# Attention, gated MLP and routed attention on one core: the first transfers in another order

## The chip, the cores and the metric

The kernel runs on one core of a Trainium2 chip. The metric is the device time of one execution in microseconds (us). Engines are named as in the profile: PE (TensorE, matmuls), DVE (VectorE), ACT (ScalarE), POOL (GpSimd) and SP, whose queue issues all transfers between HBM and the on-chip memory.

## The reference

Three layers follow one another on a batch of 2 with 448 positions. Cut to what matters:

```python
# 1. causal attention, 12 heads of width 64
scores = q @ k.T / 8, masked above the diagonal
x = softmax(scores) @ v                      # heads side by side: (2, 448, 768)
# 2. gated MLP
h = gelu(x @ w_in)                           # 1024 columns
u, v = h[..., :512], h[..., 512:]
v = layernorm(v) * g_ln
x = x + (u * (w_sg @ v + b_sg)) @ w_out
# 3. 4 attention experts of width 64, each position takes 2 of them
out = sum over e of gate[e] * softmax(causal(x wq[e] (x wk[e]).T / 8)) (x wv[e]) wo[e]
```

## The kernel before, in words

The first layer works on pairs of heads: 24 heads (two batches of 12) make 12 pairs. `qk_load` (L716) asks for q and then k of one pair, 224 KB each, into rings of two buffers per name (`qraw`, `kraw`). `qk_trans` (L728) copies such a buffer into a `pair` tile in another order (DVE, POOL or ACT, L378 to L382), and four transposes on PE (L737) turn it; the result is copied out of its PSUM bank as `qt` or `kt`. `scores1` (L771) multiplies qt and kt for both heads, in two banks per head (L782: 12 matmuls for the first bank of the pair in the trace, 8 for the second). `bank_chain` then runs per head and bank: mask, minimum and scaling on DVE (L434, into `tm` and `bias`), the exponential with its row sums on ACT (L444, into `p` and `sm`), a small step on POOL (L450), the reciprocal on DVE (L452), the scaling of p on POOL (L458) or DVE (L456), four transposes on PE (L462), and a copy into `pt` (L378 or L380). `pair_chain` multiplies pt with v for the pair (L504, 28 matmuls, called AV here) and splits the result into xh and xl.

v comes in groups of four heads, `v_group` (L700): two transfers of 64 KB (L704, L706) and three of 128 KB (L709) into one of three `v_raw` buffers. The weights of the MLP's u half come in eight transfers of 384 KB (`w_u`, L644, into three `raw` buffers); each is converted from 64-bit words to float (ACT L651, POOL L654, DVE L656 and L658) and split into a high and a low part, `wuh` and `wul` (L378 to L385). The matmuls with them (`u_chain`, L866) serve as filler on PE between the steps of the attention. Later come the v half of the MLP, the spatial product, the output product, and the third layer. `load_halves` (L877) loads g_half and b_half, which POOL scales (L885, L886).

No order is written out by hand. A planner (`class Order`, L118) runs at build time: each step names what it needs, what buffers it takes and an estimated cost; `o.add(rank, ...)` starts a chain with a rank, and among the steps that can start at about the same planned time on an engine the one of lowest rank is issued. The planner's choice fixes every engine's instruction order and, where a step allows several engines, the engine. A `need` is a condition of the planner; on the chip an instruction waits only for the data and buffers that it uses, and a transfer also for the landing of the transfer eight places ahead of it on SP's queue. The ranks of the first transfers are `4 * p + R["load"]` (that is 4p - 37) for pair p, `EARLY` (-22) for the first three weights of u, and `V0` (-4) for v's first group.

Of the kernel before, what the change touches and what calls it, by code (L numbers as in the profile page):

```python
# [105 lines left out]
def dma(ns, take=(), need=(), issue=450):  # L106
    return Step({"S": issue + 25, "A": 120 + ACTQ}, take, need, ns, issue)
# [10 lines left out]
class Order:  # L118
# [56 lines left out]
    def done(self, mark):  # L175
        self.marks[mark] = (self.t, self.e)
# [115 lines left out]
HB = 4  # L292
SIZE = dict(p32=6, pn=3, pt=6, tm=2, qraw=2, kraw=2, pair=3, qt=3, kt=3, y32=2, raw=3, w32=2, big=4)
EARLY = -22
V0 = -4


@with_exitstack
def attention_moe_kernel(
# [87 lines left out]
    def queue(e):  # L387
        return nc.sync if e == "S" else nc.scalar
# [311 lines left out]
    def v_group(g):  # L700
        b, h0 = divmod(g * HB, H)
        hs = slice(h0, h0 + HB)
        e, x = yield dma(91 * HB, ("v_raw",), [("vload", g - 1)] if g else (), issue=625)
        queue(e).dma_start(out=x[TOP, :, 0], in_=v[b, hs, 0:64, :].rearrange("h t d -> t h d"))  # L704
        e, = yield dma(91 * HB, issue=625)
        queue(e).dma_start(out=x[LOW, :, 4], in_=v[b, hs, 0:64, :].rearrange("h t d -> t h d"))  # L706
        for j in range(1, 4):
            e, = yield dma(182 * HB)
            queue(e).dma_start(  # L709
                out=x[:, :, j],  # L710
                in_=v[b, hs, 64 + P * (j - 1) : 64 + P * j, :].rearrange("h t d -> t h d"),
            )
        done(("vload", g))
        vs[g] = x

    def qk_load(p):  # L716
        b, hp = divmod(p, NP)
        raws = []
        for n, src in (("qraw", q), ("kraw", k)):
            e, t = yield dma(637, (n,), [("load", p - 1)] if p else ())  # L720
            queue(e).dma_start(
                out=t.rearrange("p h c d -> p h (c d)"),
                in_=src[b, 2 * hp : 2 * hp + 2].rearrange("h (p c) d -> p h (c d)", c=4),
            )
            raws.append(t)
        done(("load", p))
        qr, kr = raws
        o.add(4 * p + R["trans"], qk_pair(p, qr, kr))  # L728
# [14 lines left out]
    def qk_pair(p, qr, kr):  # L743
        _, qt = yield Step({"Z": 0}, ("qt",), [("qk", p - 1)] if p else ())
        _, kt = yield Step({"Z": 0}, ("kt",))
        qk[p] = (qt, kt)
        done(("qk", p))

        def k_part():
            t = yield from qk_trans(p, kr, "kraw")  # L750
            e, = yield Step(copies_ps(S), kind="ev")
            copy(e, kt, t[:, :S])
            give(BT, t)
            done(("k", p))

        o.add(4 * p + R["trans"], k_part())
        t = yield from qk_trans(p, qr, "qraw")
        e, = yield Step(copies_ps(S), kind="ev")
        copy(e, qt, t[:, :S])
        done(("q", p))  # L760
        give(BT, t)
# [147 lines left out]
    for p in range(NPAIR):  # L909
        o.add(4 * p + R["load"], qk_load(p))  # L910
        for bank in range(2):
            o.add(4 * p + bank, scores1(p, bank))
        o.add(4 * p + R["av"], pair1(p))
    for g in range(NG):
        o.add(2 * HB * g + R["vgroup"] if g else V0, v_group(g))
    for n, (ch, f) in enumerate([(0, 0), (0, 1), (1, 0), (1, 1), (0, 2), (1, 2), (0, 3), (1, 3)]):
# [545 lines left out]
```

## Time and profile before

| what | value |
|---|---|
| time, median of 3 runs | 312.5 us (311.97 to 312.9) |
| the profiled execution, its own time | 313.71 us |
| its span | 311.9 us |
| busy over the span | PE 294.0, PEld 234.0, DVE 227.4, ACT 162.4, POOL 162.8 us |
| transfers | 29.90 MB, 96 GB/s over the span |

The span is cut out of the profiled execution; what lies around it makes the difference to the execution's own time. PE is TensorE's matmuls and PEld its weight loads, which run beside them. Matmuls are pipelined, so a busy PE is not PE at its peak. PEclk is the clock that TensorE was granted, as a share of 2.4 GHz. A step in the chain of waits is named by what ran, with what released it in the line ahead of it.

### The profile page before, as it was taken

To read this page: it belongs to the slowest core of one execution; us is meant where nothing else is said; L and a number is where in the kernel's file an instruction comes from. 1 tells how busy PE (TensorE), PEld (TensorE's weight loads), DVE (VectorE), ACT (ScalarE), POOL (GpSimd) and SP (SyncE) were. 2 spreads that over 40 slices of the span, in tenths; PEclk is the share of its full clock that TensorE was granted. 3 is DMA by queue.
4 is the path that set the end of the run, shared out by engine and by line. 5 is a ranking of instruction groups with operands and counts; after the bars stand their busy time and mean duration, and the time that the engine had idled before them with its cause. 6 is when DMAs were issued, how large, how long until landed. Compare 5 with 4: busy or idle time off the path is not lost.

```text
span 311.9 us, 6208 instructions
## 1 busy us (share of the span) xinstructions
PE 294.0 (94%) x2076; PEld 234.0 (75%) x2076; DVE 227.4 (73%) x673; ACT 162.4 (52%) x423; POOL 162.8 (52%) x314
## 2 busy tenths in 40 slices
PE   6799999799999999999999999999999999986895
PEld 6467767666767789798887555999998899865794
DVE  3775876799878767727799989899966655959630
ACT  1788998798989864425466210032005335524533
POOL 4689876886987887202578860587421110112300
PEclk9589999999999999999999999999999999999999
DMA  7999456517100233314533100043101630019856
GB/s 193 211 246 232 109 147 156 139 32 221 70 12 2 69 122 86 80 34 96 141 102 102 36 19 0 0 101 78 50 25 23 115 69 17 0 26 154 144 172 202
DMA packets 55183, 29.90 MB, mean 96 GB/s; under 512 B 42800, under 2 KB 52592, under 8 KB 55152
## 3 DMA queue, kind: packets, MB, share of 16 engines
q1 hardware_dynamic: 55152, 29.52, 39.3%
q8 instruction: 16, 0.26, 0.3%
q14 instruction: 15, 0.12, 0.1%
HBM read 22.43 MB, written 2.75 MB: 81 GB/s over the span
## 4 chain that ended last, share of the span: by engine, by line
PE 72%; DMA 10%; DVE 8%; POOL 5%; issue 3%; ACT 1%; SPq 1%; DVEq 0%; ACTq 0%; POOLq 0%
PE bank L827 33%; PE bank L1061 8%; PE bank L504 6%; PE bank L782 5%; PE bank L866 5%; PE bank L1349 4%; PE bank L462 4%; DMA raw<-in_moe_w_in_dram 3%; PE bank L1310 3%; DMA pt<-pn 3%; POOL p L458 2%; DVE p L456 2%; DMA qraw<-in_q_dram 2%; PE bank L737 2%; DMA b_half<-in_moe_b_sg_dram 2%
## 5 line engine op out<-in xcount | busy, mean ns | idle before, releaser
L444 ACT ACTIVATE p<-tm,bias 128x192 f32<-128x192 f32 (+3 forms) x128 | 62.0, 503 | 12.4 <-DVE bias L434 7.9
L458 POOL TENSOR_SCALAR p<-p,sm 128x192 f32<-128x192 f32 (+1 forms) x88 | 46.2, 539 | 6.4 <-DVE sm L452 5.7
L434 DVE CUSTOM_DVE_ANT_0 tm<-bank,maskw 128x448 f32<-128x448 f32 (+2 forms) x96 | 39.3, 436 | 1.9 <-ACT p L444 1.3
L782 PE MATMUL bank<-kt,qt 64*128 64x128 f32 (+4 forms) x240 | 32.6, 397 | 2.6 <-ACT kt L378 2.6
L462 PE MATMUL bank<-ident,p 128*128 128x128 f32 x192 | 29.4, 285 | 3.1 <-POOL p L458 2.0
L782 PEld LDWEIGHTS bank<-kt,qt 64*128 64x128 f32 (+1 forms) x240 | 16.8, 193 | 15.5 <-issue 10.2
L378 ACT COPY pt<-bank 128x512 f32<-128x512 f32 x41 | 23.3, 587 | 9.5 <-PE bank L462 9.1
L462 PEld LDWEIGHTS bank<-ident,p 128*128 128x128 f32 x192 | 21.0, 142 | 9.7 <-POOL p L458 6.1
L504 PE MATMUL bank<-pt,v_raw 128*64 128x128 f32 (+3 forms) x336 | 27.4, 314 | 0.0
L504 PEld LDWEIGHTS bank<-pt,v_raw 128*64 128x64 f32 x336 | 19.8, 137 | 8.3 <-issue 4.7
L478 POOL TENSOR_SCALAR pn<-p 128x512 f16<-128x512 f32 x10 | 6.8, 678 | 33.6 <-ACT p L444 28.9
L1061 PE MATMUL bank<-wsg,vn 128*128 128x448 f32 x56 | 21.7, 539 | 0.0
L656 DVE SCALAR_TENSOR_TENSOR raw<-raw 128x384 int32<-128x384 int32 (+1 forms) x22 | 15.1, 687 | 6.2 <-POOL raw L654 6.0
L434 DVE CUSTOM_DVE_ANT_0 tm<-bank,mask 128x192 f32<-128x192 f32 x32 | 11.2, 351 | 10.1 <-PE bank L1310 6.3
L444 ACT ACTIVATION_READ_ACCUMULATOR p<-tm,bias 128x1 f32 x96 | 18.4, 192 | 0.0
L651 ACT ACTIVATE w<-raw 128x384 f32<-128x384 f32 (+1 forms) x22 | 13.0, 589 | 10.3 <-DMA raw<-in_moe_w_in_dram 6.3
L1061 PEld LDWEIGHTS bank<-wsg,vn 128*128 128x128 f32 x56 | 10.6, 190 | 10.1 <-issue 9.7
L866 PE MATMUL bank<-xh,wuh 128*128 128x448 f32 x48 | 17.9, 373 | 0.0
L866 PE MATMUL bank<-xl,wuh 128*128 128x448 f32 x48 | 17.9, 373 | 0.0
L827 PE MATMUL bank<-gh,wuh 128*128 128x448 f32 x48 | 17.9, 372 | 0.0
L654 POOL TENSOR_SCALAR raw<-raw 128x384 f32<-128x384 f32 (+1 forms) x22 | 13.3, 606 | 8.3 <-ACT w L651 7.7
L866 PE MATMUL bank<-xh,wul 128*128 128x448 f32 x48 | 17.6, 370 | 0.0
(213 smaller groups left out, 820.7 us busy)
## 6 DMA issues: line engine op xcount, KB each, us to landing
raw<-in_moe_w_in_dram SPq DMA_DIRECT2D x8, 384.0 KB, 6.1
raw<-in_moe_w_in_dram SPq DMA_DIRECT2D x6, 512.0 KB, 4.2
raw<-in_moe_w_out_dram SPq DMA_DIRECT2D x8, 384.0 KB, 3.2
qraw<-in_q_dram SPq DMA_DIRECT2D x12, 224.0 KB, 4.2
kraw<-in_k_dram SPq DMA_DIRECT2D x12, 224.0 KB, 4.6
v_raw<-in_v_dram SPq DMA_DIRECT2D x18, 128.0 KB, 4.3
out_dram<-v3r SPq DMA_DIRECT2D x3, 384.0 KB, 3.9
raw<-in_moe_w_sg_dram SPq DMA_DIRECT2D x2, 392.0 KB, 4.1
```

The lines of the kernel that those rows point to most:

```text
L378: A.copy(dst, src)
L434: V.tensor_tensor_reduce(out=tm[rs, cs], in0=s[rs, cs], in1=masks[i][rs], scale=-0.125, scalar=3.0e38, op0=ALU.add, op1=ALU.min, accum_out ...
L444: A.activation(p32[rs, cs], tm[rs, cs], AF.Exp, bias=bias[rs, i : i + 1], scale=-1.0, **({} if c.split else dict(accum_out=sm[rs, n : n + ...
L458: G.tensor_scalar(p32[rs, cs], p32[rs, cs], sm[rs, n : n + 1], 0.0, op0=ALU.mult, op1=ALU.add)
L462: T.transpose(t[:, to * P : to * P + P], p32[:, blk * P : blk * P + P], ident)
L504: T.matmul(out_, lhsT=x[:, j, :], rhs=rhs, start=(n == 0), stop=(n == len(FLIPS) - 1), skip_group_check=True)
L654: G.tensor_scalar(f32(high), f32(high), 0.0, 1.0, op0=ALU.mult, op1=ALU.mult)
L656: V.scalar_tensor_tensor(low, low, 29, high, op0=ALU.logical_shift_right, op1=ALU.bitwise_or)
L782: T.matmul(s[:m, c0 + c : c0 + c + n], lhsT=qt[rows, QCOL[i] : QCOL[i] + m], rhs=kt[rows, k0 : k0 + n], start=True, stop=True)
L827: T.matmul(o_, lhsT=a, rhs=b_, start=(i == 0), stop=(i == n - 1))
L866: T.matmul(t[:, :S], lhsT=ks[0][a], rhs=ks[1][b_], start=(c == 0 and i == 0), stop=(c == NC - 1 and i == 2))
L1061: T.matmul(t[:, :S], lhsT=vn[b][i][:, fs], rhs=w[:, ts_], start=(j == 0), stop=(j == 3))
```

## The change

Two numbers of the planner's input change. The need for the landing of the pair before is dropped for the second pair (p = 1), and the rank of v's first group goes from -4 to -30, which is ahead of the third pair (-29) and of u's first weights (-22).

```diff
-V0 = -4
+V0 = -30
...
         for n, src in (("qraw", q), ("kraw", k)):
-            e, t = yield dma(637, (n,), [("load", p - 1)] if p else ())
+            e, t = yield dma(637, (n,), [("load", p - 1)] if p > 1 else ())
             queue(e).dma_start(
```

The planner's order follows from these. PE, and SP too, have the same instructions in another order; on ACT, DVE and POOL some steps change their engine.

**SP, the first transfers.** The brackets name the semaphores that an instruction waits for (DMAHW: a landing, DVE and Pool: a release of the buffer). Before:

```order
L721 DMA qraw_197<-in_q_dram 112x2x256
L721 DMA kraw_199<-in_k_dram 112x2x256
L644 DMA raw_104<-in_moe_w_in_dram 128x3x256
L644 DMA raw_105<-in_moe_w_in_dram 128x3x256
L644 DMA raw_106<-in_moe_w_in_dram 128x3x256
L704 DMA v_raw_194<-in_v_dram 64x4x64
L706 DMA v_raw_194<-in_v_dram 64x4x64
L721 DMA qraw_198<-in_q_dram 112x2x256
L721 DMA kraw_200<-in_k_dram 112x2x256 [waits DMAHW0_49]
L709 DMA v_raw_194<-in_v_dram 128x4x64 [waits DMAHW1_49]
L709 DMA v_raw_194<-in_v_dram 128x4x64 [waits DMAHW2_49]
L709 DMA v_raw_194<-in_v_dram 128x4x64 [waits DMAHW3_49]
```

With the change:

```order
L721 DMA qraw_197<-in_q_dram 112x2x256
L721 DMA kraw_199<-in_k_dram 112x2x256
L721 DMA qraw_198<-in_q_dram 112x2x256
L721 DMA kraw_200<-in_k_dram 112x2x256
L704 DMA v_raw_194<-in_v_dram 64x4x64
L706 DMA v_raw_194<-in_v_dram 64x4x64
L709 DMA v_raw_194<-in_v_dram 128x4x64 x2
L709 DMA v_raw_194<-in_v_dram 128x4x64 [waits DMAHW0_49]
L721 DMA qraw_197<-in_q_dram 112x2x256 [waits DMAHW1_49,DVE_49]
L721 DMA kraw_199<-in_k_dram 112x2x256 [waits DMAHW2_49,Pool_49]
L644 DMA raw_104<-in_moe_w_in_dram 128x3x256 [waits DMAHW3_49]
L644 DMA raw_105<-in_moe_w_in_dram 128x3x256 [waits DMAHW4_49]
```

The second pair (`qraw_198`, `kraw_200`) comes right behind the first; all of v's first group and the third pair (again `qraw_197`, `kraw_199`) come ahead of the three weights of u. The fourth pair comes after two transfers of v's second group, in both orders.

**ACT, its first steps after the table load.** Before:

```order
L651 ACTIVATE w_107<-raw_104 128x384
L378 COPY kt_207<-bank_95 128x448
L651 ACTIVATE w_108<-raw_105 128x384
L378 CAST wuh_127<-w_107 128x384
L444 ACTIVATE p_155,sm_173<-tm_153,bias_181 128x192
```

With the change:

```order
L378 COPY qt_204<-bank_94 128x448
L378 COPY kt_207<-bank_95 128x448
L378 COPY qt_205<-bank_97 128x448
L378 COPY kt_208<-bank_98 128x448
L444 ACTIVATE p_155,sm_173<-tm_153,bias_181 128x192
```

The conversions of u's weights (L651) move from ahead of the first kt to behind the first pair's exponentials, where they stand ahead of the first copy of pt.

**PE, around the first AV product (L504).** Before, ahead of it, and then from the AV's end to the fourth pair's scores:

```order
L462 MATMUL bank_100<-ident,p_158 128x128 x4
L462 MATMUL bank_93<-ident,p_159 128x128 x4
L737 MATMUL bank_98<-ident,pair_202 128x112 x4
L737 MATMUL bank_94<-ident,pair_201 128x112 x4
L504 MATMUL bank_95<-pt_167,v_raw_194 64x384
```

With the change:

```order
L462 MATMUL bank_93<-ident,p_157 128x128 x4
L737 MATMUL bank_96<-ident,pair_201 128x112 x4
L737 MATMUL bank_97<-ident,pair_203 128x112 x4
L462 MATMUL bank_99<-ident,p_158 128x128 x4
L782 MATMUL bank_93<-kt_209,qt_206 128x448
L782 MATMUL bank_96<-kt_209,qt_206 128x448
L782 MATMUL bank_93<-kt_209,qt_206 64x64
L782 MATMUL bank_96<-kt_209,qt_206 64x64
L504 MATMUL bank_99<-pt_167,v_raw_194 64x384
```

In both, the two groups of L737 ahead of the AV are the fourth pair's. With the change the second bank of the third pair's scores (`kt_209`, `qt_206`) moves ahead of the AV. Behind the AV stand, with the change:

```order
L462 MATMUL bank_95<-ident,p_159 128x128 x4
L737 MATMUL bank_97<-ident,pair_202 128x112 x4
L462 MATMUL bank_100<-ident,p_155 128x128 x4
L462 MATMUL bank_98<-ident,p_160 128x128 x4
L866 MATMUL bank_95<-xh_75,wuh_127 128x448
L866 MATMUL bank_95<-xl_81,wuh_127 128x448
L866 MATMUL bank_95<-xh_75,wul_131 128x448
L782 MATMUL bank_99<-kt_207,qt_204 128x128
```

The last row is the first matmul of the fourth pair's scores. Before, no L866 stands ahead of it, and one group of L737 more. The `p_155` in the third row is scaled on DVE (L456), behind three passes of L434 and one conversion step of a weight (L656).

## Rows read from the trace of the kernel before

**Rows 1.** Busy time of each engine in stretches (start:end, length, then busy us).

```profile
25.70:60.00 34.30, 32.60 (x307) 23.22 (x308) 24.95 (x104) 30.05 (x93) 27.56 (x62) 1.00 0.66 163
60.00:275.00 215.00, 213.42 (x1290) 170.62 (x1286) 167.12 (x450) 103.44 (x258) 114.31 (x202) 1.00 0.24 62
275.00:312.00 37.00, 27.39 (x360) 24.97 (x360) 19.42 (x60) 13.90 (x31) 4.58 (x6) 1.00 0.64 147
```

**Rows 2.** The same view early: PE, PEld, DVE, ACT, POOL, PEclk, DMA share, GB/s.

```profile
5.00:8.40 3.40, 1.44 (x12) 1.10 (x10) 0.62 (x1) 0.65 (x2) 0.17 (x2) 0.98 1.05 293
8.40:18.50 10.10, 8.76 (x44) 5.86 (x46) 7.16 (x26) 7.53 (x23) 7.10 (x14) 0.50 1.12 209
```

**Rows 3.** The chain that ended last, at the start: start us, us, what.

```profile
1.68 6.05 DMA raw<-in_moe_w_in_dram
...
8.30 0.43 ACT kt L378
...
8.77 2.34 PE bank L782 x12
```

**Rows 4.** SP's queue in order of time: k of the first, second, fourth pair.

```profile
1.20 0.44 SPq L721 DMA_DIRECT2D kraw<-in_k_dram  x1
...
6.01 0.47 SPq L721 DMA_DIRECT2D kraw<-in_k_dram  x1
...
14.92 0.32 SPq L721 DMA_DIRECT2D kraw<-in_k_dram  x1
```

**Rows 5.** Transfers, last column us to landing: the same three, in that order.

```profile
kraw<-in_k_dram SPq DMA_DIRECT2D x1, 224.0 KB, 3.3
...
kraw<-in_k_dram SPq DMA_DIRECT2D x1, 224.0 KB, 7.8
...
kraw<-in_k_dram SPq DMA_DIRECT2D x1, 224.0 KB, 5.6
```

**Rows 6.** What SP's queue waited for up to 14 us (total, times, longest).

```profile
SPq L721 <- DMA raw<-in_moe_w_in_dram: 0.8, 1, 0.8
```

**Rows 7.** Timeline of DVE; groups by form (mean ns after the comma); chain pieces.

```profile
22.72 0.41 DVE L380 COPY pair<-kraw 112x512 f32<-112x512 f32 x1
...
L658 DVE SCALAR_TENSOR_TENSOR w<-w,raw 128x384 int32<-128x384 int32 x8 | 5.6, 705 | 0.1
L656 DVE SCALAR_TENSOR_TENSOR raw<-raw 128x384 int32<-128x384 int32 x8 | 4.7, 590 | 5.3 <-POOL raw L654 5.2
L380 DVE COPY qt<-bank 128x448 f32<-128x448 f32 x5 | 3.1, 619 | 1.6 <-PE bank L737 1.6
...
100.77 0.35 DVE tm L434
...
101.12 0.40 DVE tm L434
...
101.64 1.64 DVE p L456 x2
```

**Rows 8.** The chain on PE from the first AV on, and four fillers.

```profile
25.78 2.21 PE bank L504 x28
...
28.59 1.21 PE bank L782 x8
29.80 0.59 PE bank L462 x4
30.39 0.77 PE bank L737 x8
31.16 1.19 PE bank L782 x12
...
58.06 0.82 PE bank L866 x4
```

**Rows 9.** Timelines of POOL and PE around 55 us, with idle time before and releaser.

```profile
53.61 0.62 POOL L886 TENSOR_SCALAR b_half<-b_half 128x512 f32<-128x512 f32 x1 [0.75 <-DMA b_half<-in_moe_b_sg_dram]
...
56.64 0.65 PE L462 MATMUL bank<-ident,p 128*128 128x128 f32 x4 [1.70 <-POOL p L458]
```

## The prediction, made before the changed kernel was run

> **What bounds the kernel now.** I read the stretches first, the TensorE timeline of the start next, then the chain of waits, and last the transfers. The table of stretches says where TensorE (PE) is the limit: from 25.7 us to 275 us it is busy 246.0 of 249.3 us, and from 275 us to the end only 27.4 of 37.0 us [rows 1]. So in the long middle, work that starts earlier on PE ends earlier, and the loss sits at the two ends. The change is at the first. There the clock row shows a loss of its own: between 5.0 and 8.4 us PE is busy 1.44 of 3.4 us, and from 8.4 to 18.5 us it has a granted clock of 0.50, the lower level of 1.2 GHz [rows 2]. The reader is to see in the chain why PE stood still before: the first transfer of u's weights, issued at 1.68 us, takes 6.05 us to land; ScalarE (ACT) converts it first and only then copies kt of the first pair, so the first scores begin at 8.77 us although q and k of that pair had landed by 4.5 us (1.20 + 3.3) [rows 3 to 5].
>
> The second pair comes late too. Its k transfer is issued at 6.01 us and lands 7.8 us later, at 13.8 us; that of the fourth pair is issued at 14.92 us and lands at 20.5 us [rows 4, 5]. The transfers stand in a line: between those two landings came the three whole blocks of v's first group (384 KB), the third pair (448), two half blocks of v's second group (128) and the fourth pair (448), 1,408 KB in 6.7 us, 210 KB per us. The SP queue, which issues them, stood for 0.8 us because of a landing of w_in [rows 6]: in the listing each transfer waits for the one eight places ahead of it.
>
> **The change, part by part.** *It removes no wait on the chip.* The need that is dropped is one of the planner's; the listing of SP in the section on the change shows that q of the second pair had no semaphore to wait for, only five transfers ahead of it: three of u's weights (1,152 KB) and two of v (128 KB). What is changed is the order, and from it every engine's order in the first hundred microseconds; no instruction of PE is added or removed.
>
> *Second pair earlier.* Ahead of its last byte now stand 448 KB, not 1,728 KB. At 210 KB per us its k lands at 4.5 + 448/210 = 6.6 us instead of 13.8 us. DVE's copy (0.41 us) and two groups of transposes (0.77 us for eight matmuls) follow [rows 7, 8], so PE goes on at about 7 us, and the first scores, which stand behind those transposes, start near 7.8 us, 1 us earlier than at 8.77 us. ACT copies qt and kt with no weight ahead of them. PE is then busy for about 2.6 of the 3.4 us in which it was busy 1.44 us [rows 2], and I take it that the clock stays at 2.4 GHz. Third pair: 4.5 + 1,408/210 = 11.2 us.
>
> *v's first group earlier.* Its 512 KB now stand ahead of the third pair; that costs 2.4 us of landing there, which is covered, since PE has the scores of two pairs (2.4 us each) until then. It gains nothing by itself: the first use of v is the AV product at 25.78 us [rows 8].
>
> *u's weights later.* Three transfers move behind the third pair and end near 16.7 us (4.5 + 2,560/210). They are needed only by filler matmuls. But ACT converts the first two ahead of its first copy of pt, so that copy comes after the second weight's landing, 4.5 + 2,176/210 = 14.9 us; with two steps of ACT and one group of L462, 0.6 us each (an estimate by the 0.59 of L462 and of L656 [rows 7, 8]), PE is through with all it can do without the fourth pair at 16.7 us.
>
> *Fourth pair: unchanged.* Before its last byte 3,584 KB have been asked for in both orders (4 pairs of 448, three weights of 384, v's first group of 512 and two halves of 64 of the second). All through this stretch the queues are full (DMA share over 1.0 [rows 2]), so I let it land at 20.5 us as before, 4 us after PE has run out of work. In the kernel before, its transposes came just ahead of the AV product at 25.78 us, so it was not waited for. This landing is what is late next, and sets the sum:
> - DVE copies k: 20.5 + 0.41 = 20.9 us. PE: four transposes 0.39, four of L462 0.59, the second bank of scores 1.21, AV 2.21, L462 0.59, four transposes 0.39: 26.3 us [rows 7, 8].
> - DVE, meanwhile, from 20.9 us in its new order: one L658 0.71, a copy of qt 0.62, three mask passes of 0.75 (0.35 + 0.40), one L656 0.59, the two L456 that scale p 1.64, and 0.4 for reciprocals between them (an estimate from the row gaps): 27.2 us [rows 7]. PE's next group reads this p, so PE waits 0.9 us.
> - PE then does two groups of L462 (1.18) and three filler matmuls (0.62, from 0.82 for four) and starts the scores of the fourth pair at 29.0 us, against 31.16 us before: 2.2 us [rows 8].
> - At that point PE has done the same as before, but for three fillers more (0.62) and one group of four transposes less (0.39): 0.2 us. Gain at the head: **2.4 us**.
>
> Bounds of that landing: if landing kept pace with what the DMA moved (293 GB/s to 8.4 us, 209 after that [rows 2]), the 3,584 KB would be in at some 18.6 us, 1.9 us sooner. If one transfer of w_in more slipped ahead, it would be 384/210 = 1.8 us later. I take 20.5 us, because it was measured with the same bytes ahead.
>
> *Later stretches.* Two unknowns of opposite sign. At 56.64 us PE loses 1.70 us to POOL, which had been waiting for b_half [rows 9]; POOL's scaling of b_half now stands 15 instructions later in its order, so between 0 and 1.7 us may come back. On the other side, at 29 us one weight conversion more is still to be done, 1.3 us of DVE (0.59 + 0.71 [rows 7]), in a stretch where ACT is busy 30.05 of 34.3 us [rows 1]: 0 to 1.3 us lost. I count the two against each other at zero and keep their ends. From the v projection to the third stage PE's order is the same row by row; in the tail one group of four transposes of y stands elsewhere, which I cost at nothing: it lies in 9.6 us of idle PE time [rows 1], with both signs possible.
>
> Sum against the profiled execution: its span of 311.9 us becomes 309.5 us; it took 313.71 us in all, so 311.3 us. The median of the runs shown, 312.5 us, becomes **310.1 us**.
>
> **Rivals.**
> (a) *The transfers keep pace* and the fourth pair is there 1.9 us sooner, and b_half's stall goes too: 2.4 + 1.9 + 1.7 = 6.0 us, 306.5 us. For it: the DMA moved 293 GB/s between 5.0 and 8.4 us [rows 2]. Against: the same bytes.
> (b) *The helpers set the pace.* ACT, DVE and POOL are busy 88, 73 and 80% between 25.7 and 60 us [rows 1], and their work is not less. If PE, coming earlier, meets p that is late again as at 27.2 us, a second and a third wait of 0.9 us and the 1.3 us of conversion eat the gain: 2.4 - 1.8 - 1.3 = -0.7 at the worst, so 312 to 313 us, no change. Against: what they missed between 5 and 10 us is also won.
> (c) *The clock falls at a new place: slower.* From 16.7 to 20.9 us PE has nothing to do but wait for the fourth pair. The trace shows what such a wait does: after the idle before 8.77 us the clock was 0.50 for 10.1 us [rows 2, 3]. If the same follows from 21 us on, PE's steps up to 31.1 us take twice as long, and the scores of the fourth pair start near 33.2 us (5.1 us of the 7.2 us of PE work from 20.9 us on is done by 31.1 us): 2.0 us later than before, 0.2 of it made up by the fillers, so 314.3 us. The loss is half the low stretch, less the 0.9 us that hide behind DVE; above 6.6 us at the low clock (3.3 - 0.9 = 2.4) the change is slower. A short fall, of 3 us, costs 0.6 us and lies in the forecast's range. Against a long one: PE's work after 21 us is dense, where before it was broken by waits for the second pair. The Trainium skill, in "TensorE: Matmul & The Clock Gate", section "HAM oscillation — how this bites in real kernels", says that a wait for DMA between pieces of matmul work makes the clock drop and the next piece start cold. By that rule (c) would be the result; the trace agrees at 8.4 us (0.50), while idle stretches like the 1.70 us at 56.64 us left the clock at 1.00 [rows 1, 9].
> (d) *The change does nothing*, since the pieces ahead of the AV are tied by p and not by transfers: 312.5 us. Against it stands the chain, in which the first scores wait for a landing [rows 3].
>
> **How the numbers follow.** Forecast (308.9 to 311.5 us) 0.45; (a) 0.18; (b) 0.18; (c) 0.16; (d) 0.03. A measurement of this kernel tells about 0.3% from no change, here 0.94 us. Faster by more than that: the forecast (0.45), (a) and 0.01 of (b): 0.64. Within it: the rest of (b) and (d): 0.20. Slower: (c), 0.16. The range goes from (a), 306.5 us, to the top of (b), 313.0 us; (c) above that and a larger gain than (a) are left out.
>
> **What the profile of the changed kernel would show.** Right: first scores near 7.8 us; granted clock 1.00 through 8.4 to 18.5 us; k of the second pair landed by 7 us and of the fourth near 20.5 us; PE idle for up to 4 us before 21 us; the first AV at about 23 us instead of 25.78 us; PE as dense as before from 30 to 275 us. Wrong: a clock of 0.50 after 20 us (c), a fourth pair landed by 19 us (a), new idle of PE before L462 between 27 and 60 us with POOL or DVE as what ended it (b), or a first AV no earlier than 25 us (d).

## The result and the profile after the change

The changed kernel takes 308.36 us (median of 4 runs, 308.17 to 309.04) against 312.4 us beside it: a ratio of 0.9874 with a 95% interval of 0.9852 to 0.9895. Forecast were 310.1 us (308.9 to 311.5 us) and faster: the way was right, and the time lies just below that band. Run twice more among the experiments it gave 0.9875 [0.9855, 0.9895] and 0.9866 [0.9834, 0.9899].

| | before | after |
|---|---|---|
| the profiled execution | 313.71 us | 309.04 us |
| its span | 311.9 us | 307.2 us |
| scores of the fourth pair start (chain) | 31.16 us | 28.79 us |
| first product of the spatial step, L1061 (chain) | 169.92 us | 165.15 us |
| last 42 matmuls of the output, L1349 (chain) | 300.97 us | 296.30 us |

The last two rows of before are these pieces of its chain:

```profile
169.92 24.05 PE bank L1061 x64
...
300.97 7.29 PE bank L1349 x42
```

So of 4.7 us of span 2.4 us are won by the fourth pair's scores, 2.4 us more on the way to L1061, and from there to the end nothing changes. By medians 4.0 us are won: the profiled execution of before was 1.3 us above its median, that of after 0.7 us.

The stretches of after, in the columns of [rows 1, 2] (length, PE, PEld, DVE, ACT, POOL, PEclk, DMA share, GB/s):

```profile
5.00:8.40 3.40, 3.09 (x20) 2.35 (x19) 0.43 (x1) 1.36 (x3) 0.94 (x2) 1.00 1.30 205
8.40:18.50 10.10, 8.94 (x76) 5.49 (x74) 6.19 (x32) 7.45 (x25) 5.03 (x13) 1.00 1.16 249
...
25.70:60.00 34.30, 33.52 (x302) 23.77 (x302) 28.98 (x109) 30.40 (x92) 30.17 (x62) 1.00 0.66 164
60.00:275.00 215.00, 213.69 (x1335) 170.66 (x1334) 164.79 (x452) 101.43 (x252) 116.44 (x206) 1.00 0.24 62
275.00:307.00 32.00, 25.00 (x287) 23.24 (x283) 15.22 (x48) 14.49 (x33) 4.73 (x6) 0.95 0.73 170
```

PE is busy 3.09 us from 5.0 to 8.4 us instead of 1.44, and from 8.4 to 18.5 us at the full 2.4 GHz it does 76 matmuls of the records where it did 44 at 1.2 GHz [rows 2]. Between 25.7 and 60 us it is busy 33.52 instead of 32.60 us [rows 1]: 0.9 us more, in a stretch where the prediction had set gain and loss against each other at zero. In the tail the clock is below 1.00.

The chain after, at its start and at the landmarks (start, length, what), against [rows 3, 8]:

```profile
1.68 5.03 DMA qraw<-in_q_dram
...
7.19 5.29 DMA kraw<-in_k_dram
...
18.93 2.01 POOL p L458 x2
...
25.04 1.01 DVE raw L656
...
28.79 1.19 PE bank L782 x12
...
165.15 24.05 PE bank L1061 x64
...
296.30 7.30 PE bank L1349 x42
```

The first landing in it is now that of the second pair's q, not a weight. Then comes the third pair's k, and after that helpers: two scalings of p on POOL (L458), a step of a weight's conversion on DVE (L656). The timeline of PE gives the same from PE's side, with the idle time ahead and who ended it:

```profile
8.65 3.46 PE L782 MATMUL bank<-kt,qt 64*128 64x128 f32 x32
...
18.99 0.60 PE L737 MATMUL bank<-ident,pair 112*128 112x112 f32 x4 [0.53 <-POOL pair L382]
19.90 0.57 PE L737 MATMUL bank<-ident,pair 112*128 112x112 f32 x4 [0.31 <-DVE pair L380]
21.00 0.66 PE L462 MATMUL bank<-ident,p 128*128 128x128 f32 x4 [0.52 <-POOL p L458]
...
22.80 2.29 PE L504 MATMUL bank<-pt,v_raw 128*64 128x384 f32 x28
...
26.72 1.35 PE L462 MATMUL bank<-ident,p 128*128 128x128 f32 x8 [0.49 <-DVE p L456]
```

SP's queue: k of the second and of the fourth pair are issued at

```profile
2.18 0.46 SPq L721 DMA_DIRECT2D kraw<-in_k_dram  x1
...
11.59 0.50 SPq L721 DMA_DIRECT2D kraw<-in_k_dram  x1
```

and their rows among the transfers (last column us to landing) are, in that order,

```profile
kraw<-in_k_dram SPq DMA_DIRECT2D x1, 224.0 KB, 5.3
...
kraw<-in_k_dram SPq DMA_DIRECT2D x1, 224.0 KB, 7.4
```

So the second pair's k landed at 7.5 us and the fourth's at 19.0 us, against 13.8 and 20.5 us before [rows 4, 5]. One more place matters. POOL's scaling of b_half, which waited 1.15 us for g_half and 0.75 us [rows 9] for b_half before, stands later in POOL's order and waits for nothing (timeline of POOL):

```profile
61.22 0.63 POOL L886 TENSOR_SCALAR b_half<-b_half 128x512 f32<-128x512 f32 x1
```

### The profile page after: what moved, and what is told of

Its sections match the earlier page's. It is cut to its first block, busy times and chain, and to the rows that moved or that the text cites. A ratio compares the mean times of both kernels' runs of the same rounds, so it can differ in the third digit from the quotient of the medians.

```text
span 307.2 us, 6207 instructions
## 1 busy us (share of the span) xinstructions
PE 294.0 (96%) x2076; PEld 233.0 (76%) x2076; DVE 223.5 (73%) x668; ACT 162.3 (53%) x424; POOL 166.9 (54%) x319
## 4 chain that ended last, share of the span: by engine, by line
PE 80%; POOL 7%; DMA 6%; DVE 3%; issue 2%; ACT 0%; POOLq 0%; SPq 0%; DVEq 0%
PE bank L827 34%; PE bank L866 9%; PE bank L1061 8%; PE bank L462 6%; PE bank L782 6%; PE bank L504 6%; POOL p L458 4%; PE bank L1349 4%; PE bank L1310 3%; DMA pt<-pn 2%; DMA kraw<-in_k_dram 2%; DMA qraw<-in_q_dram 2%; PE bank L737 1%; PE bank L976 1%; DVE tm L434 1%
## 5 line engine op out<-in xcount | busy, mean ns | idle before, releaser
L458 POOL TENSOR_SCALAR p<-p,sm 128x448 f32<-128x448 f32 (+1 forms) x86 | 46.6, 555 | 7.4 <-DVE sm L452 5.9
L434 DVE CUSTOM_DVE_ANT_0 tm<-bank,maskw 128x448 f32<-128x448 f32 (+2 forms) x96 | 39.2, 435 | 1.3 <-ACT p L444 1.1
L378 ACT COPY pt<-bank 128x512 f32<-128x512 f32 x46 | 25.9, 586 | 9.6 <-PE bank L462 8.9
L782 PE MATMUL bank<-kt,qt 64*128 64x128 f32 (+4 forms) x240 | 30.1, 370 | 0.0
L504 PE MATMUL bank<-pt,v_raw 128*64 128x128 f32 (+3 forms) x336 | 27.4, 314 | 0.0
L462 PEld LDWEIGHTS bank<-ident,p 128*128 128x128 f32 x192 | 20.9, 140 | 7.7 <-POOL p L458 3.8
L504 PEld LDWEIGHTS bank<-pt,v_raw 128*64 128x64 f32 x336 | 19.7, 137 | 9.0 <-issue 5.5
L782 PEld LDWEIGHTS bank<-kt,qt 64*128 64x128 f32 (+1 forms) x240 | 15.0, 175 | 12.0 <-issue 10.0
L1061 PE MATMUL bank<-wsg,vn 128*128 128x448 f32 x56 | 21.7, 539 | 0.0
L656 DVE SCALAR_TENSOR_TENSOR raw<-raw 128x384 int32<-128x384 int32 (+1 forms) x22 | 17.3, 790 | 5.5 <-POOL raw L654 5.5
L444 ACT ACTIVATION_READ_ACCUMULATOR p<-tm,bias 128x1 f32 x96 | 18.5, 193 | 0.0
L1061 PEld LDWEIGHTS bank<-wsg,vn 128*128 128x128 f32 x56 | 10.6, 190 | 10.1 <-issue 9.5
L866 PE MATMUL bank<-xh,wuh 128*128 128x448 f32 x48 | 18.2, 380 | 0.0
L866 PE MATMUL bank<-xl,wuh 128*128 128x448 f32 x48 | 18.1, 377 | 0.0
L654 POOL TENSOR_SCALAR raw<-raw 128x384 f32<-128x384 f32 (+1 forms) x22 | 14.0, 639 | 7.2 <-ACT w L651 6.4
L434 DVE CUSTOM_DVE_ANT_0 tm<-bank,mask 128x192 f32<-128x192 f32 x32 | 11.1, 348 | 9.1 <-PE bank L1310 6.3
L866 PE MATMUL bank<-xh,wul 128*128 128x448 f32 x48 | 17.8, 373 | 0.0
L827 PE MATMUL bank<-gl,wuh 128*128 128x448 f32 x48 | 17.5, 365 | 0.0
```

The lines of the kernel that those rows point to most:

```text
L378: A.copy(dst, src)
L434: V.tensor_tensor_reduce(out=tm[rs, cs], in0=s[rs, cs], in1=masks[i][rs], scale=-0.125, scalar=3.0e38, op0=ALU.add, op1=ALU.min, accum_out ...
L444: A.activation(p32[rs, cs], tm[rs, cs], AF.Exp, bias=bias[rs, i : i + 1], scale=-1.0, **({} if c.split else dict(accum_out=sm[rs, n : n + ...
L458: G.tensor_scalar(p32[rs, cs], p32[rs, cs], sm[rs, n : n + 1], 0.0, op0=ALU.mult, op1=ALU.add)
L462: T.transpose(t[:, to * P : to * P + P], p32[:, blk * P : blk * P + P], ident)
L504: T.matmul(out_, lhsT=x[:, j, :], rhs=rhs, start=(n == 0), stop=(n == len(FLIPS) - 1), skip_group_check=True)
```

## The experiments

Theory: the second pair's early landing, with engine orders made for it, gives the gain at the head; the rest comes from the stall at b_half. Rivals: the clock, the landing alone, the orders alone, v's place alone.

**1. Warm-up in the kernel before.** Is the low clock of [rows 2] a cause that can be removed by itself?

```diff
 def work(n, need):
-        for _ in range(n):
+        for _ in range(n if n == WARM else n + 9):
             T.matmul(t[:, :P], lhsT=zeros, rhs=zeros, start=True, stop=True)
```

> The kernel before with nine more warm-up matmuls on PE ahead of the first scores, all orders else the same. They fill PE's idle time from 6.5 to 8.8 us, so the clock should not fall at 8.4 us. Theory of the clock (the start lost its time because PE ran at 0.50 from 8.4 to 18.5 us): up to half of the 8.8 us of busy time there comes back, 308 to 309 us. Theory of the arrival (PE waits for the second pair, which lands at 13.8 us, whatever the clock): PE only waits longer for it; 0 to 1 us, 311.4 to 312.4 us.

Measured: ratio to before 1.0017 [0.9987, 1.0046]. The timeline of PE and the stretches of this kernel:

```profile
13.45 0.60 PE L737 MATMUL bank<-ident,pair 112*128 112x112 f32 x4 [2.82 <-POOL pair L382]
```

```profile
14.00:15.00 1.00, 0.65 (x5) 0.58 (x4) 0.76 (x1) 0.53 (x1) 1.00 (x2) 0.77 0.94 214
15.00:18.00 3.00, 2.96 (x17) 2.04 (x16) 0.93 (x3) 2.47 (x7) 2.31 (x7) 0.50 1.12 224
```

PE runs through the first scores at full clock, then stands 2.82 us for the second pair, and the clock falls behind that wait: 0.50 from 15 to 18 us, where PE is busy 2.96 of 3.00 us. So the nine matmuls moved the low stretch and did not remove it. Up to the second pair's landing the low clock of before had cost little of its own: PE came to that pair's transposes at 13.84 us before and at 13.45 us here, since the landing set the time. What it costs behind the landing this run doesn't show. The kernel of experiment 6, whose order is that of before in this stretch, had the clock at 1.00 in a part of it:

```profile
13.00:16.00 3.00, 1.47 (x10) 1.06 (x11) 2.94 (x12) 2.56 (x10) 2.77 (x6) 1.00 0.81 219
```

Its first AV began at 25.59 us, against 25.71 us before and 26.11 us here (timelines of PE). No gain is seen, but no profile of this order has the clock at 1.00 throughout, so how much of the gain at the head comes with the clock stays open.

**2 and 3. The landing without the orders, and the orders without the landing.** In the kernel before, only the place of the second pair's transfers is changed:

```diff
-            queue(e).dma_start(
+            if p != 1:
+                queue(e).dma_start(
...
+        if p == 0:
+            for n, src in (("qraw", q), ("kraw", k)):
+                (_, _, t), = o.rings[n]
+                nc.sync.dma_start(
```

> The kernel before, with every engine's order as it was, and only q and k of the second pair asked for right behind the first pair's. Theory that the order of the transfers alone carries the gain: 308.4 to 310 us. Theory that it needs the engines' order with it: the second pair lands near 7.5 us and waits, since ACT still converts u's first weight ahead of the first kt, and that weight now lands some 2 us later, so the first scores start near 10.8 us instead of 8.77 us: 312 to 313.5 us.

In the changed kernel, only u's three weights are asked for ahead of the second pair again:

```diff
-        queue(e).dma_start(out=raw[:, : 2 * n].rearrange("p (a b) -> p a b", a=shape[0]), in_=src)
+        asked[0] += 1
+        if asked[0] > 3:
+            queue(e).dma_start(out=raw[:, : 2 * n].rearrange("p (a b) -> p a b", a=shape[0]), in_=src)
...
+        if p == 0:
+            for (_, _, raw), (ch, f) in zip(o.rings["raw"], ((0, 0), (0, 1), (1, 0))):
+                nc.sync.dma_start(
```

> The changed kernel with the order of every engine but SP's left as it is: u's three weights (1,152 KB) are asked for right behind the first pair, ahead of the second pair, as in the kernel before. Theory (the second pair's early landing carries the gain at the head, and the engines' orders are only good because of it): the second pair's k lands about 5 us later than 7.5 us, at 12.5 to 13.5 us, first scores no sooner than 14 us since the second pair's transposes stand ahead of them on PE, the first AV near 26 us or later, 311.5 to 314 us. Rival (the gain comes from the engines' new orders, and the transfers have slack): first AV within 1 us of 22.8 us, 308.4 to 309.5 us. Either way the stretch from 60 to 170 us stays as in the changed kernel, so that up to 2 us of the 4.1 us may remain: then about 311 us.

Measured: 1.0042 [1.0017, 1.0067] for the first, 1.0084 [1.0063, 1.0106] for the second, both slower than the kernel before. In the first the second pair's k landed at 2.18 + 5.5 = 7.7 us, as in the changed kernel, but on ACT the copy of kt still stood behind a weight's conversion (timeline of PE; lines are eight further down here):

```profile
9.61 4.19 PE L790 MATMUL bank<-kt,qt 64*128 64x128 f32 x20 [2.77 <-ACT kt L378]
14.68 1.76 PE L745 MATMUL bank<-ident,pair 112*128 112x112 f32 x8 [0.87 <-POOL pair L382]
...
25.95 2.29 PE L504 MATMUL bank<-pt,v_raw 128*64 128x384 f32 x28
```

The first scores were expected near 10.8 us and began at 9.61 us. The data of the second pair was there, and DVE, ACT and PE came to it no sooner. The first AV is 0.2 us later than before (25.95 against 25.71 us); where the rest of the 0.4% goes this profile doesn't show. In the second, k of that pair landed at 3.78 + 8.1 = 11.9 us, and PE, whose order puts its transposes ahead of all scores, stood for it (lines ten further down):

```profile
11.53 1.94 PE L747 MATMUL bank<-ident,pair 112*128 112x112 f32 x8 [2.72 <-POOL pair L382]
13.40 4.99 PE L792 MATMUL bank<-kt,qt 64*128 64x128 f32 x32
...
29.07 2.84 PE L504 MATMUL bank<-pt,v_raw 128*64 128x384 f32 x28
```

Neither half gives anything alone; the wrong order of transfers under the new engine orders is the dearest combination, 2.3 us over before.

**4 and 5. Each edit alone.** The need alone (V0 stays at -4), and v's rank alone (the need stays):

> The kernel before with the first of the two edits alone: the need is dropped for the second pair, v's rank stays at -4. The second pair is asked for right behind the first, then u's weights, v and the third pair mixed. Theory (the second pair's landing, with engine orders made for it, carries the head's gain; v's rank alone is worth little): second pair's k landed by 7.6 us, first scores before 9 us, 308.5 to 310 us. Rival (ACT's conversion of u's first weight, whose transfer now lands ahead of v and the third pair, keeps its place ahead of the copies of kt, so both edits are needed): first scores after 9 us, 311.5 to 313 us.

> The kernel before with the second of the two edits alone: v's first group (512 KB) is asked for right behind the first pair, and the second pair still waits in the plan for the first one's landing, so it comes behind v and ahead of u's weights. Theory (what counts is that the second pair is in before PE has run out of the first one's work): its k lands about 2.4 us later than with both edits (512 KB at 210 KB per us), near 10 us, first scores near 11 us, between the kernel before and the changed one: 309.5 to 312 us. Rival (v's place carries something of its own, since v_raw is then there early): no slower than the changed kernel, 308.2 to 309.3 us.

Measured: the need alone 0.9881 [0.9857, 0.9905], the same as both edits; v alone 0.9961 [0.9934, 0.9988]. PE in the kernel with the need alone:

```profile
8.69 4.47 PE L782 MATMUL bank<-kt,qt 64*128 64x128 f32 x40
...
22.82 2.29 PE L504 MATMUL bank<-pt,v_raw 128*64 128x384 f32 x28
...
26.82 1.25 PE L782 MATMUL bank<-kt,qt 64*128 64x128 f32 x12
```

So one edit carries the whole gain. With it the planner put the copies of the first pair's qt and kt ahead of the conversions though u's weights were still asked for at 2.68 us, which the rival had doubted. With v alone the second pair's k landed at 5.43 + 4.7 = 10.1 us, as expected, but first scores near 11 us were wrong: the planner put the first pair's scores ahead of the second pair's transposes, so they began at 6.65 us, and PE then had too little to do; the stretches show the clock at 0.50:

```profile
12.00:14.00 2.00, 1.92 (x12) 1.39 (x12) 0.67 (x5) 1.77 (x8) 1.83 (x5) 0.50 1.19 219
```

First AV at 24.28 us, fourth-pair scores at 30.38 us: between the two kernels, as is the time. In this kernel too POOL's scaling of b_half comes later, at 59.84 us, and waits for nothing; so its 0.4% are not the head's alone.

**6 and 7. The stall at b_half.** POOL's scaling of g_half and b_half is taken out of its place and emitted after a count of other steps: in the kernel before 71 POOL instructions later, in the changed kernel 19 earlier, so that it meets the landing of b_half again (there the count stands behind the small step of L450 and is 3; lines five further down).

```diff
+            if late:
+                late[0] -= 1
+                if late[0] == 0:
+                    G.tensor_scalar(g_half, g_half, 0.5, 0.0, op0=ALU.mult, op1=ALU.add)
+                    G.tensor_scalar(b_half, b_half, 0.5, 0.0, op0=ALU.mult, op1=ALU.add)
...
-        G.tensor_scalar(g_half, g_half, 0.5, 0.0, op0=ALU.mult, op1=ALU.add)
-        G.tensor_scalar(b_half, b_half, 0.5, 0.0, op0=ALU.mult, op1=ALU.add)
+        late.append(20)
```

> The kernel before, with only POOL's scaling of g_half and b_half moved some 70 instructions later on POOL. Theory that the wait for b_half at 53.6 us is a loss of its own, apart from the start: PE's wait of 1.70 us at 56.6 us goes, 310.7 to 311.1 us. Rival: POOL's next late p takes its place and PE waits the same: 312.4 us.

> The changed kernel with POOL's scaling of g_half and b_half moved some 19 instructions ahead in POOL's order, so that POOL waits for b_half's landing near 51.5 us as it did in the kernel before; all else stays. Theory (about 2 us of the 4.1 us come from this stall being gone): a wait of PE for p scaled on POOL of 1 to 2 us between 51 and 57 us, 0.7 to 2 us slower than the changed kernel, 309.2 to 310.6 us. Rival (POOL has slack there now, and the 2 us come from elsewhere): within 0.5 us of the changed kernel, 308.2 to 309.1 us.

Measured: without the stall the kernel before takes 0.9975 [0.9952, 0.9998] of its time, 0.7 us less by medians. With a stall the changed kernel takes 309.23 us, 0.9900 [0.9869, 0.9931], against 308.45 us for itself in the same job, 0.9866 [0.9834, 0.9899]: 0.8 us, though these intervals overlap. The waits of PE between 25 and 140 us (total, times, longest) were in the kernel before

```profile
PE bank L462 <- POOL p L458: 1.7, 1, 1.7
PE bank L462 <- DVE p L456: 0.8, 2, 0.5
PE bank L976 <- DVE wvnl L385: 0.6, 1, 0.6
```

and without the stall there

```profile
PE bank L467 <- DVE p L456: 0.8, 2, 0.5
```

in the changed kernel

```profile
PE bank L462 <- POOL p L458: 0.7, 3, 0.3
PE bank L462 <- DVE p L456: 0.5, 1, 0.5
```

and with the stall put back

```profile
PE bank L467 <- POOL p L463: 1.7, 2, 0.9
```

A stall of 1.91 us on POOL (timelines of POOL and PE in the last of these kernels) does come out on PE as a wait for p, and the wait is shorter than the stall:

```profile
51.38 0.62 POOL L455 TENSOR_SCALAR b_half<-b_half 128x512 f32<-128x512 f32 x1 [1.91 <-DMA b_half<-in_moe_b_sg_dram]
```

```profile
52.96 1.56 PE L467 MATMUL bank<-ident,p 128*128 128x128 f32 x12 [0.92 <-POOL p L463]
```

So the stall's end is a gain of its own, and the two runs size it at 0.7 to 0.8 us. From the fourth pair's scores to L1061 single profiles give more: 138.8 us before, 136.2 us without the stall (31.03 to 167.19), 136.4 us in the changed kernel. Why so much more than the 0.7 us of the medians? One profiled execution is a sample. The kernels of experiments 1 and 2 have the same orders on PE and POOL here, with the stall at b_half in it, and the wait that it leaves on PE was shorter in their profiles than the 1.7 us of before, first experiment 1, then 2:

```profile
PE bank L462 <- POOL p L458: 0.6, 1, 0.6
```

```profile
PE bank L462 <- POOL p L458: 1.1, 1, 1.1
```

On POOL the stall itself was 1.90 us in the profile of before (1.15 for g_half and 0.75 for b_half), 1.34 us in experiment 1 and 1.10 us in experiment 2, and the two scalings of p behind it took 1.87, 1.24 and 1.87 us. Experiment 1 has no wait at L976 either, and from the fourth pair's scores to L1061 it takes 136.9 us (31.55 to 168.41). So the stall left PE a wait of 0.6 to 1.7 us in three executions, and the profile of before shows the longest.

**8. The fourth pair sooner.** In the changed kernel the need is dropped for the third and the fourth pair too, so that the fourth pair comes ahead of u's weights.

```diff
-            e, t = yield dma(637, (n,), [("load", p - 1)] if p > 1 else ())
+            e, t = yield dma(637, (n,), [("load", p - 1)] if p > 3 else ())
```

> The changed kernel with the same need dropped for the third and the fourth pair as well: q and k of the fourth pair are asked for ahead of u's three weights. Theory (the fourth pair's landing at 19.0 us sets the first AV): it lands up to 5 us sooner, PE has no wait near 18 to 21 us, the scores of the fourth pair start 1 to 2 us before 28.8 us, 306.5 to 307.5 us if what is won stays won. Rival 1 (the helpers ACT, DVE and POOL set the pace by then): fourth-pair scores within 0.5 us of 28.8 us, 308.4 us. Rival 2 (u's weights come too late, and their conversions then collide with the exponentials between 25 and 60 us): 309 to 311 us.

Measured: 0.9882 [0.9861, 0.9902], the same as the changed kernel. The fourth pair's k landed at 7.66 + 5.5 = 13.2 us, 5.8 us sooner, and its scores began at 26.58 us; but a new wait came up, and the lead was gone by L1061 (164.59 us in the chain; the changed kernel has 165.15, 164.42 and 164.78 us in its three profiles). PE and the chain of that kernel:

```profile
19.97 0.66 PE L462 MATMUL bank<-ident,p 128*128 128x128 f32 x4 [1.63 <-POOL p L458]
...
26.58 1.25 PE L782 MATMUL bank<-kt,qt 64*128 64x128 f32 x12
```

```profile
164.59 24.05 PE bank L1061 x64
```

The fourth pair's scores came 2.2 us sooner, which rival 1 had denied, but the time is that of the changed kernel, as rival 1 gave it. Behind the scores the way to L1061 takes 138.0 us, against 136.4, 136.6 and 136.2 us in the three profiles of the changed kernel, and from 26 to 165 us PE is idle for 1.9 us, against 1.3, 0.9 and 0.5 us. Between 25 and 140 us it waits for POOL (p and pair, 1.0 us) and DVE (pair and p, 0.7 us). So the landing at 19.0 us is no longer the bound, and a good part of the lead is lost to the helpers; the rest is not accounted for.

**9. Fewer warm-ups in the changed kernel.** Eight of the ten matmuls of zeros at the start are left out; they add nothing to the output.

```diff
-        for _ in range(n):
+        for _ in range(1):
```

> The changed kernel with 8 of its 10 warm-up matmuls left out, all orders else the same; the clock should fall before the first scores. Theory of the clock: the low clock through the dense work from 7.5 to 18.5 us costs half of its 9 us and more, 311.5 to 313 us. Theory of the arrival: PE has slack before the fourth pair's landing at 19.0 us, and only what is beyond it is lost: 308.4 to 310.5 us.

Measured: 310.38 us, 0.9923 [0.9900, 0.9947], slower by about 0.5% than the changed kernel in the other jobs (0.9875 [0.9855, 0.9895]). Its profiled execution (309.04 us) shows none of it: clock 1.00 from 5.0 to 18.5 us, first AV at 21.88 us, L1061 at 164.24 us. Of its eleven executions seven had a mean clock of 0.989 and took 309.8 to 310.7 us, four had 0.992 to 1.0 and took 308.6 to 309.5 us. That points to a clock that falls in most of them. But the changed kernel itself took 308.2 to 309.1 us at mean clocks of 0.986 and 0.989, so a low mean alone does not make the loss; where the clock fell here no profile shows, and the cause stays open.

**10. The clock in the tail.** In the changed kernel the clock fell in the tail, so twelve matmuls are put into the bank that the next transposes overwrite.

```diff
         _, t = yield op(T=436, take=(BT,), need=need)
+        splits.append(mark)
+        for _ in range(12 if len(splits) == 1 else 0):
+            T.matmul(t[:, :P], lhsT=ident, rhs=ident, start=True, stop=True)
```

> The changed kernel with twelve extra matmuls of the identity (128 columns each) ahead of the first transposes of y in the third layer, into the bank that these transposes then overwrite; they lie in PE's wait before 277 us. In two profiles of the changed kernel the granted clock fell to 0.50 between 277 and 285 us, behind a stretch in which PE was busy for under half of the time. Theory (the sparse work makes the clock fall, and the fall costs time in the tail): clock 1.00 from 276 to 290 us, 0.5 to 1.5 us faster, 307.1 to 308.1 us. Rival 1 (the tail is bound by DVE and the transfers of pt, not by PE's clock): clock stays up but the time is within 0.4 us of the changed kernel. Rival 2 (the extra matmuls don't fit in the wait): slower, 309 to 310 us.

The changed kernel itself ran beside 3, 4 and 8 (the first text) and beside 5, 7 and 10 (the second):

> The changed kernel once more, so that the three kernels beside it are compared with it under the same conditions. Every theory: 308.2 to 309.2 us, ratio to before 0.985 to 0.990. In the profile the first scores near 8.65 us, the scores of the fourth pair near 28.8 us.

> The changed kernel a third time, as the measure for the two kernels that are made from it: 308.2 to 309.2 us, ratio to before 0.985 to 0.990 by every theory.

Measured: with the matmuls 309.17 us, 0.9904 [0.9870, 0.9938]; the changed kernel 308.45 us in that job, 308.62 us in the other. A stretch of the tail and PE's wait behind it, first in the changed kernel (third time):

```profile
278.00:280.00 2.00, 1.39 (x26) 1.22 (x24) 0.99 (x3) 0.98 (x3) 0.00 (x0) 0.50 1.17 152
```

```profile
284.31 0.20 PE L523 MATMUL bank<-v3s,pt 128*128 128x65 f16 x1 [1.29 <-DMA pt<-pn]
```

then in the one with twelve matmuls more:

```profile
278.00:280.00 2.00, 1.29 (x43) 1.17 (x40) 0.90 (x3) 1.54 (x4) 0.00 (x0) 1.00 0.99 157
```

```profile
284.11 0.20 PE L523 MATMUL bank<-v3s,pt 128*128 128x65 f16 x1 [1.56 <-DMA pt<-pn]
```

The clock stayed at 1.00, and PE waited 1.56 instead of 1.29 us for the same transfer of pt. The span is 307.4 us against 306.9 us. In these two profiles the tail waits for the transfers of pt at either clock, as rival 1 says. The time, though, is 0.7 us above the changed kernel's, in the range of rival 2, and its reason is there too: the twelve matmuls took 2.92 us where PE had waited 1.96 us, and the transposes of y began at 277.36 instead of 276.80 us. The intervals overlap, so what the twelve matmuls cost is not shown; that they gain nothing is. No version was found that beats the changed kernel.

## Why the prediction came out right, and where its steps were off

The direction and the mechanism at the head held: 310.1 us were forecast, 308.4 us measured, with the fourth pair's scores at 28.79 us where 29.0 us stood in the sum and the first AV at 22.80 instead of 23.1 us. The size did not: 308.4 us lie inside the whole range (306.5 to 313.0 us) but below the forecast's own band (308.9 to 311.5 us), in the part that was given to rival (a), and 4.0 us were won where 2.4 us were added up. Point by point:

- *"It removes no wait on the chip."* Held: asking earlier does nothing by itself (experiment 2). What the dropped need changes is every engine's order; the early landing and the orders are needed together (experiments 2, 3).
- *Second pair.* Its landing was sized too early, 7.5 instead of 6.6 us: from 4.5 to 7.5 us its 448 KB came at 150 KB per us, not at 210. First scores therefore at 8.65 us, not 7.8 us, and hardly sooner than 8.77 us. That cost nothing, because what counts is what follows: the scores of both pairs then run together, 3.46 us for 32 matmuls at full clock, and PE is not left without work.
- *PE through at 16.7 us, then idle for up to 4 us.* PE had work until 18.5 us, and up to 21.0 us it waited 0.53, 0.31 and 0.52 us. A part of its idle time lay earlier: the third pair's k landed at 12.5 us (7.19 + 5.29), not at 11.2, and PE waited 0.95 us for that pair's transposes at 13.05 us.
- *Clock.* 1.00 through 8.4 to 18.5 us, as taken.
- *v's group "gains nothing by itself".* On top of the need it brings nothing (0.9881 without it, 0.9875 with it in one job). Alone it gains 0.4%: u's weights go behind the second pair, the fourth pair's scores come 0.7 us sooner, and b_half's stall is gone there too. Which of these gives how much is not shown.
- *"Fourth pair: unchanged ... I let it land at 20.5 us".* It landed at 19.0 us, near the lower bound of 18.6 us (whose sum leaves out what was moved from 4.5 to 5.0 us; with it the bound is nearer to 18 us). The reason given, the same bytes ahead, was too weak: the queues moved 249 GB/s from 8.4 to 18.5 us where they moved 209 before [rows 2]. Its gain was eaten on the way: the scores came 9.8 us after the landing, not 8.5. In the chain two scalings of p on POOL take 2.01 us, and the DVE step L656 1.01 us where 0.59 us was the mean [rows 7]. Two errors of 1.3 to 1.5 us cancelled: that the sum came within 0.2 us of the fourth pair's scores is luck.
- *PE's wait for DVE's p.* 0.9 us forecast, 0.49 us at 26.72 us. (DVE's steps from 20.9 us add up to 27.1 us, not 27.2.)
- *"I count the two against each other at zero"* is the step that failed. Of its two ends, the return of b_half's stall was real: 0.7 to 0.8 us by experiments 6 and 7. The 1.70 us that stood as its end were read from one profile; in two others with the stall in the same place PE lost 0.6 and 1.1 us. The other, 1.3 us of DVE's conversion as a loss, is not seen in PE's waits: those for p scaled on DVE came to 0.5 us between 25 and 140 us, all of it at 26.72 us, and to 0.8 us before.

Added up from runs: the head, 31.09 us before against 28.72, 27.83 and 28.58 us in the three timelines of the changed kernel, is 2.4 to 3.3 us, with 0.2 us of work done more; the stall gives 0.7 to 0.8 us. That makes 3.3 to 4.3 us, and 4.0 us were measured.

Of the rivals, (a) named the right direction of the miss, a fourth pair that lands sooner and b_half's stall gone, but not its size: experiment 8 shows that landings of the fourth pair before 19 us are worth nothing. (b), helpers that set the pace, is what stopped further gain, not what took the gain away. (d) fell with the result. (c), the clock that falls after the wait for the fourth pair, did not happen in the profile of the result, but it did in another of the same kernel. Stretches of the third profile of the changed kernel:

```profile
21.00:22.00 1.00, 1.00 (x6) 0.48 (x4) 1.00 (x5) 0.79 (x2) 0.92 (x2) 0.59 0.90 278
...
23.00:24.00 1.00, 1.00 (x8) 0.48 (x10) 0.73 (x6) 1.00 (x5) 0.75 (x4) 0.50 0.91 219
24.00:25.00 1.00, 1.00 (x8) 0.49 (x6) 0.55 (x2) 1.00 (x6) 1.00 (x2) 0.70 1.03 282
```

The clock is at its lower level for some 3 us, the length that the prediction had priced at 0.6 us; the AV takes 2.92 instead of 2.29 us, yet the fourth pair's scores begin at 28.58 us and the span is 306.9 us. Of the six profiles with this head (experiments 7, 9, 10 and three of the changed kernel) two show it, this one and that of experiment 7. The Trainium skill ("TensorE: Matmul & The Clock Gate", section "HAM oscillation — how this bites in real kernels") has the next piece of work start cold after a wait for DMA. In these two it did, behind single waits of at most 0.53 us from 18 to 21 us here and of 1.01 us in experiment 7; the other four, with waits of 0.46 to 0.54 us in the same place, stayed at 1.00. The fall that came was too short to turn the sign.

## What to carry to other kernels

A transfer that comes earlier is worth only what the engines' orders let it be: look at who stands ahead of its first consumer on each engine, and change both, or neither. Count the steps that a new plan happens to move past a wait elsewhere: a helper's stall 30 us behind the change was here a fifth of the gain. And where two unknowns of opposite sign are set against each other at zero, go back to the waits of the engine that bounds: here they showed a wait that could return, and none from which the loss could grow. Read the size of such a wait in more than one profile: this one was 1.7, 1.1 and 0.6 us in three executions of the same orders.

## What the runs showed of the hardware that was not expected

- The same order of work had TensorE's clock at 1.00 behind the waits near 20 us in four profiles and at 0.50 for about 3 us in two, and what follows a landing moved by close to 1 us from one execution to the next (the fourth pair's first transposes at 18.99, 18.06 and 18.52 us in the three profiles of the changed kernel). Neither shows in the time: spans of 307.2, 306.8 and 306.9 us.
- A clock of 0.50 does not have to cost: the third profile of the changed kernel had it for some 3 us at 21 to 25 us and again in the tail, and its span of 306.9 us is no longer than the 307.2 us of the first, which had it in the tail alone.
- A wait for the same two small landings (g_half, b_half) held POOL for 1.90, 1.34 and 1.10 us in three executions (before, experiments 1 and 2) and PE behind it for 1.7, 0.6 and 1.1 us, while the spans were 311.9, 310.7 and 311.6 us.
